# Gated linear attention followed by a sine MLP: the MLP's first weight fetched in four column quarters, with a new instruction order

## The chip, the cores and the metric

The kernel runs on one core of a Trainium2 chip. The metric is the device time of one execution in microseconds (us), as the median of several runs; lower is better. A profile of one execution comes with it, and all times inside the program are counted from the start of its span.

## The reference

Two stages follow each other. The first is a recurrence over 768 time steps for 4 batches of 8 heads with head size 48; its output, put token by token (3072 tokens of 384 numbers), goes through an MLP whose activation is `h + sin(alpha*h)^2 / alpha`.

```
f = 1 / (1 + exp(-f_logit))                       # [4, 8, 768, 48]
for t in range(768):
    state = f[:, :, t, :, None] * state + k[:, :, t] (outer) v[:, :, t]
    y[:, :, t] = q[:, :, t] @ state
x = y as [3072, 384]
h = x @ w_in                                      # [3072, 2048]
g = h + sin(alpha * h)^2 / (alpha + 1e-9)
out = g @ w_out                                   # [3072, 384]
```

## The kernel before

The sequence is cut into six chunks of 128 steps. Within a chunk the recurrence is turned into matrix products: sums of log gates (`cs`, a product with a triangular mask), the scaled `k` and `q` (`kh` and `qh`, both in the tile `qk`), their transposes (`tp`, copied to `tr`), the masked score matrix (`aps`, masked into `at`), the product with `v` (`y`, copied to `yn`), and the state carried to the next chunk (`kv`, `st`). `y` is transposed once more (`yt`, copied to `xT`) and is then the input of the MLP for the 512 tokens of this chunk (128 steps of 4 batches).

The work of `pre` is done for two batches at a time; such a unit is `u = 2*chunk + pair`, so u 0 and 1 are chunk 0, u 2 and 3 are chunk 1, and so on. A unit needs four inputs `f`, `k`, `q`, `v`, each a 384 KB DMA issued by the SyncE queue (SP) in the order that the list `LOADS` gives. Below, v2 means the `v` input of unit 2. `kh`, `qh`, `tp`, `tr`, `aps`, `at` and `kv` are made for one batch at a time, numbered m = 2*u + 0 or 1: kh2 and kh3 come from k1, kh4 and kh5 from k2. Each kind of input has three buffers.

The MLP of a chunk has 16 blocks of 128 hidden columns (`fb`). For each block: three matmuls into `h` (`first`, L543), the sine on ScalarE (L548), the square on GpSimd, ScalarE or VectorE (L554, L556), and the sum into `g` on VectorE (L561). In chunk 0 the blocks are done for two batches (256 tokens) at a time, so that chunk 0 has 32 of them; h0 to h15 are those of its first two batches. `second` multiplies `g` with `w_out` (L581) into `o`, which is copied to `osb` and stored. `h` has three PSUM buffers in turn; in chunk 0 some of the first 15 blocks use the two buffers of `o` as well.

The weights come over the GpSimd queue (POOL), since they are cast from float32 to bfloat16 on the way. Each group of these DMAs is gated: a copy of one element of an input tile into `seen` (L286) waits until that input has landed, and the DMAs stand behind it in the POOL queue. `W_GATE` tells which entries of `LOADS` are the gates of the first part of `w_in`, of its second part, and of `w_out`. In the kernel before, one half of `w_in` is three DMAs, one for each 128 rows, and a block of the second half (`fb` 8 to 15) needs all three of its half:

```python
W_GATE = [4, 7, 14]
w_in_dma[hf].append(op(rank, {POOL: 600}, emit, deps=[gate], dma=1660))
needs = lambda half, fb: [...] + w_in_dma[fb // 8]
```

The order of the instructions on every engine is made while the program is built. `op` records each operation with a rank, the engines that it may run on with a planned cost, and what it depends on; `in_order` then plays them through with these costs and takes again and again the operation that can start first, rank and `BIAS` deciding ties. So planned costs and ranks set which engine does a copy or a square, and the place of every instruction. The result is a fixed order on each engine, and on the chip each engine works its own queue in that order. `PHASES` sets when ScalarE turns between exponentials and sines, which takes a table load (L643).

Of the kernel before, what the change touches and what calls it, by code (L numbers as in the profile page):

```python
# [22 lines left out]
LOADS = [("f", 0), ("k", 0), ("q", 0), ("f", 1), ("q", 1), ("v", 0), ("k", 1), ("v", 1), ("q", 3),  # L23
    ("f", 2), ("v", 2), ("f", 3), ("k", 4), ("q", 2), ("k", 2), ("v", 3), ("k", 3), ("f", 4),
    ("f", 5), ("v", 4), ("q", 4), ("v", 7), ("q", 5), ("f", 7), ("k", 5), ("k", 6), ("v", 5),
    ("q", 8), ("f", 6), ("f", 8), ("q", 6), ("k", 7), ("v", 6), ("k", 8), ("v", 8), ("v", 10),
    ("v", 9), ("k", 10), ("q", 7), ("f", 10), ("v", 11), ("q", 10), ("f", 11), ("k", 9), ("q",
    9), ("k", 11), ("q", 11), ("f", 9)]
W_GATE = [4, 7, 14]
LAG = [1259, 664, 156, 107, 352, 821]  # L30
ATT = [816, -410, -264, -308, -540, 67]
# [3 lines left out]
RANK = [57, 902, -416, 116, 324, -1107, 154, -228, -393, 499, -57, -21]  # L35
MULS = {"POOL": 1020, "DVE": 750}
KIND = {"v": [-253, -197, -275, -90, -19, -113, 54, -23, 294, 108, -136, 11],
        "cs": [166, -99, 466, 468, 497, 525, 156, 73, 308, 100, -174, -211],
        "kh": [-420, -288, -109, -60, -261, -416, 1, 112, -116, -353, -597, -410],
        "qh": [39, -59, -267, -207, -95, -105, -79, -204, -36, -58, 106, 145],  # L40
        "tp": [-704, -587, -407, -250, -350, -423, -529, -434, -209, -113, -630, -619],
        "tr": [676, 683, 605, 574, 597, 434, 658, 637, 516, 502, 841, 893],
        "a": [-193, -33, -307, -268, -491, -499, -415, -297, -236, -148, -542, -369],
        "m": [382, 244, 882, 926, 455, 521, 870, 880, 558, 664, 209, 409],
        "y": [359, 281, 782, 934, 738, 726, 967, 789, 882, 759, 797, 900],
        "yt": [338, 442, 591, 498, 369, 453, 920, 776, 936, 571, 725, 839],
        "xe": [164, 118, 474, 430, 628, 568, 660, 448, 819, 638, 731, 791],
        "i": [-178, -9, -130, -85, -385, -454, -347, -676, -80, 105, -145, 51],
        "kv": [105, 140, -54, 56, 130, -66, -209, -24, 56, 108, 260, 93],
        "st": [-156, -144, -34, 68, -433, -296, -147, -222, -33, 60, -123, -22],  # L50
        "h": [-282, -193, -192, -427, -22, -104, -640, -227, -306, -284, -211, -314],
        "sq": [110, -5, -368, -360, -77, -233, -538, -538, -402, -388, -227, -18],
        "g": [-196, -86, -99, -320, -310, -185, -65, -203, 63, 30, -333, -448],
        "ev": [98, 89, -544, -601, -357, -242, -98, -190, -420, -283, -225, -463]}
ON_ACT = {"tr": [164, -107, -316, 43, -634, 114, -467, 93, 3854, -711, -8369, -5250],
          "y": [-1550, -3600, -3600, -14550, -10950, -650, 1050, -4550, -350, -5050, 3650, 100],
          "xe": [5550, 6200, -5450, 2700, 200, -100, 4250, 6900, 4000, 6850, 2600, 2800],
          "sq": [200, 900, 10400, -1400, -450, 450, -100, -1000, -250, 7250, -250, 12600],
          "ev": [7850, 12700, 3150, 2350, 850, 50, -5400, -700, 3000, 9250, 8600, -1850]}
BIAS = {"ACT": 500, "DVE": 500, "POOL": 600, "SP": 200}  # L60
# [25 lines left out]
def in_order(ops, lines):  # L86
# [28 lines left out]
    while left:  # L115
# [20 lines left out]
        if o.dma:  # L136
            dma_free[e] = max(s + 600, dma_free[e]) + o.dma
            o.end = dma_free[e] + DMA_LATENCY
            if e == "POOL":
                dma_free["SP"] = max(s + 600, dma_free["SP"]) + o.dma  # L140
# [18 lines left out]
def kernel(  # L159
# [18 lines left out]
    nc = tc.nc  # L178
# [38 lines left out]
    def op(rank, engs, emit, deps=(), takes=(), holds=(), table=None, dma=None):  # L217
        o = Op(rank, engs, emit, [d for d in deps if d is not None], list(takes), table, dma)
        for b in list(takes) + list(holds):
            b.users.append(o)  # L220
        ops.append(o)
        return o
# [55 lines left out]
    HF = [slice(0, d_ff // 2), slice(d_ff // 2, d_ff)]  # L278
# [3 lines left out]
    w_in_dma, w_out_dma = {0: [], 1: []}, {}  # L282
# [6 lines left out]
    def w_in_load(hf, rank):  # L289
        gate = weights_after(hf, rank)  # L290
        for kb in range(KB):
            def emit(e, kb=kb):
                nc.gpsimd.dma_start(out=w_in_bf[:, kb, HF[hf]], in_=moe_w_in[kb * P:(kb + 1) * P, HF[hf]])
            w_in_dma[hf].append(op(rank, {POOL: 600}, emit, deps=[gate], dma=1660))
# [27 lines left out]
    def pre(u, rank):  # L322
# [15 lines left out]
        l = op(rank, {ACT: 790}, ln_, deps=[x], takes=[lf], holds=[fb_], table=EXP)  # L338
        act = [x, l]
        made["v", u] = op(rank + KIND["v"][u] + 2, {DVE: 870}, values, deps=[vb_.ready], takes=[vv], holds=[vb_])  # L340
        late = []
        for i in range(2):
# [34 lines left out]
            c_ = op(rank + KIND["cs"][u] + i, {PE: 170 if last else 370}, cs_, deps=[l], takes=[cb], holds=[lf])  # L377
# [8 lines left out]
            made["qh", m] = op(rank + KIND["qh"][u] + i, {DVE: 490}, qm, deps=[g, qb_.ready], takes=[qkb], holds=[qb_, cb])  # L386
            if not last:
                made["gl", m] = op(rank + i, {DVE: 110}, gl_, deps=[g], takes=[glb], holds=[cb])
# [3 lines left out]
    def attend(c, b, rank):  # L392
# [96 lines left out]
        if c < PE_TR:  # L489
            kt = op(rank + KIND["tp"][u], {PE: 250}, lambda e: tp_(e, 0), deps=[made["kh", m]], takes=[tpb], holds=[qkb])  # L490
            qt = op(rank + KIND["tp"][u], {PE: 250}, lambda e: tp_(e, 1), deps=[made["qh", m], kt], holds=[tpb, qkb])
            tr = op(rank + KIND["tr"][u], {DVE: 640, ACT: 970}, tr_, deps=[qt], takes=[trb], holds=[tpb])
            tr.on_act = ON_ACT["tr"][u]
        else:
            tr = op(rank, {SP: 1300}, tr_, deps=[made["kh", m], made["qh", m]], takes=[trb], holds=[qkb], dma=3000)
        a = op(rank + KIND["a"][u], {PE: 400}, a_, deps=[tr], takes=ab + atb, holds=[trb])
        ms = [op(rank + KIND["m"][u], {DVE: 640}, lambda e, r=r: m_(e, r), deps=[a], holds=[ab[r], atb[r]]) for r in range(2)]
        last_ = None
        if not first:
            last_ = op(rank + KIND["i"][u], {PE: 210}, inter_, deps=[a, made["st", c - 1, b]], takes=[yb], holds=[trb, sold])  # L500
        for r in range(2):
            last_ = op(rank + KIND["i"][u], {PE: 170}, lambda e, r=r: intra_(e, r), deps=[ms[r], last_, made["v", u]],
                       takes=[yb] if first and r == 0 else [], holds=[yb, atb[r], vb])
        y_op = op(rank + KIND["y"][u], {DVE: 520, ACT: 430}, y_, deps=[last_], takes=[ynb], holds=[yb])
        y_op.on_act = ON_ACT["y"][u]
        if c < Y_TR:
            yt = op(rank + KIND["yt"][u], {PE: 200}, yt_, deps=[y_op], takes=[ytb], holds=[ynb])
            made["x", c, b] = op(rank + KIND["xe"][u], {DVE: 300, ACT: 440}, x_, deps=[yt], takes=[xb], holds=[ytb])
            made["x", c, b].on_act = ON_ACT["xe"][u]
        else:  # L510
            made["x", c, b] = op(rank + KIND["xe"][u], {SP: 1300}, yt_, deps=[y_op], takes=[xb], holds=[ynb], dma=1200)
        if not last:
            sold_op = made.get(("st", c - 1, b))
            if c < SUM:
                kv = op(rank + KIND["kv"][u] + 1, {PE: 200 if first else 370}, kv_, deps=[made["kh", m], made["v", u], sold_op],
                        takes=[kvb, sb], holds=[qkb, vb] + ([sold] if sold else []))
                made["st", c, b] = op(rank + KIND["st"][u] + 1, {DVE: 520}, st_, deps=[kv, made["gl", m]],
                                      holds=[sb, kvb, bufs["gl", m]])
            else:
                kv = op(rank + KIND["kv"][u] + 1, {PE: 200}, kv_, deps=[made["kh", m], made["v", u], sold_op],  # L520
                        takes=[kvb, sumb, sb], holds=[qkb, vb])
                su = op(rank + KIND["st"][u] + 1, {DVE: 520}, sum_, deps=[kv, sold_op], holds=[sumb, kvb, sold])
                made["st", c, b] = op(rank + KIND["st"][u] + 1, {POOL: 800, DVE: 710}, st_, deps=[su, made["gl", m]],
# [4 lines left out]
    def first(c, fb, ts, rank, needs):  # L528
# [39 lines left out]
        s = op(rank, {ACT: 455 if half else 645}, sin_, deps=[a, made["al"]], takes=[sb], holds=[hb], table=TRIG)  # L568
        t = op(rank + KIND["sq"][w], {POOL: 640 if half else 1040, ACT: 420 if half else 640, DVE: 520 if half else 917}, sq, deps=[s], takes=[s2b], holds=[sb])
        t.on_act = ON_ACT["sq"][w]  # L570
        made["g", c, fb, ts.start] = op(rank + KIND["g"][w], {DVE: 420 if half else 685}, add, deps=[t], takes=[gb], holds=[s2b, hb])
        return s

    def second(c, t, rank):
# [18 lines left out]
        v_ = op(rank + KIND["ev"][2 * c + t // 2], {DVE: 520, ACT: 500}, ev, deps=[prev], takes=[sbuf], holds=[ob])  # L593
# [17 lines left out]
    needs = lambda half, fb: [made["x", 0, 2 * half + i] for i in range(2)] + w_in_dma[fb // 8]  # L611
# [63 lines left out]
```

## Time and profile before

| What | us |
|---|---|
| median of 4 runs | 220.51 |
| the runs | 219.59 to 221.26 |
| the profiled execution's own time | 221.26 |
| its span, first to last instruction | 219.6 |
| TensorE (PE) busy | 182.9 |
| VectorE (DVE) busy | 160.2 |
| ScalarE (ACT) busy | 163.6 |
| GpSimd (POOL) busy | 100.3 |
| DMAs of `w_in`, issue to landing, shortest / median / longest | 4.7 / 7.2 / 8.1 |

The profiled execution is the slowest of the four runs, 0.75 us over the median; 1.66 us of its own time lie outside the span. The busy times are sums over the whole span: what a wait costs has to be read where it stands. "q1" in the lists of DMA queues is the queue that SP fills (inputs, stores, DMA transposes), "q0" is the one that POOL fills (`alpha`, `w_in`, `w_out`); their columns are packets, MB written, and the time of the packets as a share of the 16 DMA engines in that stretch, which exceeds 100% where packets overlap.

### The profile page before, as it was taken

Reading aid. Unit: us, or ns where it says so; the run is one execution under the profiler, and the core shown is the slowest. Engines: PE = TensorE matmul, PEld = TensorE weight load, DVE = VectorE, ACT = ScalarE, POOL = GpSimd, SP = SyncE. Lnnn points to the kernel's source line nnn. Section 1 sums busy time; section 2 is a strip of 40 time slices with the busy share of each in tenths; the row PEclk is TensorE's granted clock in tenths of the full one; section 3 lists DMA queues with packets and bytes.
Section 4 is the critical chain, followed back from the end, with each engine's and each line's share of the span. In section 5 each row is a group of like instructions: output and inputs, shape, how many; then the busy total and the mean of one; then the engine's idle time right before and its main releaser. Section 6 shows DMA issues by size and latency. Waiting matters only on the chain.

```text
span 219.6 us, 4284 instructions
## 1 busy us (share of the span) xinstructions
PE 182.9 (83%) x1537; PEld 108.0 (49%) x1537; DVE 160.2 (73%) x297; ACT 163.6 (75%) x269; POOL 100.3 (46%) x129
## 2 busy tenths in 40 slices
PE   0468545845999997896999988997999999999993
PEld 0347423524677564454565444554554555555551
DVE  2387762827689579988968998849899968787820
ACT  3565443897578997699998898998898888687601
POOL 5332441848255358867566645377604312302300
PEclk9999955755699999999999999999999999999999
DMA  7999999999998999979949999486302211001121
GB/s 130 187 188 189 181 174 180 190 202 190 210 186 161 200 184 181 186 113 188 222 93 138 187 186 217 127 159 130 109 18 40 91 25 69 0 36 72 37 74 72
DMA packets 118997, 30.30 MB, mean 138 GB/s; under 512 B 113072, under 2 KB 118208, under 8 KB 118976
## 3 DMA queue, kind: packets, MB, share of 16 engines
q1 hardware_dynamic: 115968, 26.88, 69.3%
q0 software_dynamic: 3008, 3.15, 9.2%
q8 instruction: 12, 0.20, 0.4%
q14 instruction: 9, 0.07, 0.1%
HBM read 25.17 MB, written 4.72 MB: 136 GB/s over the span
## 4 chain that ended last, share of the span: by engine, by line
PE 49%; ACT 13%; DVE 10%; issue 8%; POOL 7%; SPq 5%; DMA 5%; POOLq 0%; ACTq 0%
PE o L581 23%; PE h L543 19%; POOL s L556 6%; SPq L270 5%; DMA v<-in_v_dram 5%; DVE g L561 5%; ACT s L548 3%; ACT L643 3%; ACT Gi L364 2%; DVE at L429 2%; PE aps L426 2%; ACT lf L331 1%; ACT f L328 1%; PE tp L409 1%; ACT cs L360 1%
## 5 line engine op out<-in xcount | busy, mean ns | idle before, releaser
L556 POOL TENSOR_TENSOR s<-s 128x512 f32<-128x512 f32 (+1 forms) x67 | 58.8, 893 | 68.6 <-ACT s L548 44.0
L548 ACT ACTIVATE s<-h,al_p 128x512 f32<-128x512 f32 (+1 forms) x112 | 67.7, 626 | 27.8 <-PE h L543 23.3
L543 PE MATMUL h<-xT,w_in_bf 128*128 128x512 bf16 (+1 forms) x336 | 79.5, 362 | 10.4 <-DMA w_in_bf<-in_moe_w_in_dram 6.0
L561 DVE SCALAR_TENSOR_TENSOR g<-s,al_r,h 128x512 bf16<-128x512 f32 (+1 forms) x112 | 72.2, 667 | 10.7 <-POOL s L556 6.8
L581 PE MATMUL o<-w_out_bf,g 128*128 128x384 bf16 x384 | 78.5, 329 | 0.0
L543 PEld LDWEIGHTS <-w_in_bf 128*128 128x128 bf16 x336 | 33.1, 102 | 37.4 <-DMA w_in_bf<-in_moe_w_in_dram 7.3
L581 PEld LDWEIGHTS <-g 128*128 128x128 bf16 x384 | 35.7, 98 | 23.5 <-issue 0.7
L429 DVE TENSOR_TENSOR at<-aps,mask 128x512 bf16<-128x512 f32 x48 | 31.7, 684 | 5.0 <-PE aps L426 4.8
L373 POOL TENSOR_TENSOR qk<-k,Gi 128x384 bf16<-128x384 f32 x22 | 21.9, 1015 | 22.3 <-ACT Gi L364 19.9
L373 DVE TENSOR_TENSOR qk<-q,cs 128x384 bf16<-128x384 f32 x24 | 13.1, 552 | 13.2 <-ACT cs L360 12.5
L554 ACT ACTIVATE s<-s 128x512 f32<-128x512 f32 (+1 forms) x34 | 20.8, 614 | 0.8
L351 PE MATMUL cs<-lf,mask 128*128 128x384 bf16 x24 | 8.6, 377 | 9.8 <-ACT lf L331 8.6
L446 PE MATMUL y<-vb,at 128*128 128x48 bf16 x192 | 11.5, 187 | 4.7 <-DVE vb L335 2.8
L409 PE MATMUL tp<-ident,qk 128*128 128x128 bf16 x128 | 12.2, 259 | 3.3 <-POOL qk L373 1.9
L446 PEld LDWEIGHTS <-at 128*128 128x128 bf16 x192 | 8.9, 98 | 10.9 <-DVE at L429 5.2
L643 ACT ACT_TABLE_LOAD x11 | 14.1, 1283 | 0.2
L328 ACT ACTIVATE f<-f 128x768 f32<-128x768 f32 x12 | 10.1, 838 | 5.1 <-DMA f<-in_f_logit_dram 5.0
L556 DVE TENSOR_TENSOR s<-s 128x512 f32<-128x512 f32 (+1 forms) x11 | 7.8, 708 | 7.7 <-ACT s L548 7.6
L364 ACT ACTIVATE Gi<-cs 128x384 f32<-128x384 f32 x24 | 11.6, 485 | 2.0 <-PE cs L354 1.9
L426 PE MATMUL aps<-tr 64*128 64x128 bf16 x192 | 11.0, 229 | 2.5 <-ACT tr L417 1.5
L417 ACT COPY tr<-tp 128x1024 bf16<-128x1024 bf16 x10 | 9.9, 1019 | 3.9 <-PE tp L409 3.9
L409 PEld LDWEIGHTS <-qk 128*128 128x128 bf16 x128 | 10.4, 118 | 4.9 <-POOL qk L373 2.6
(54 smaller groups left out, 155.9 us busy)
## 6 DMA issues: line engine op xcount, KB each, us to landing
f<-in_f_logit_dram SPq DMA_DIRECT2D x12, 384.0 KB, 7.3
k<-in_k_dram SPq DMA_DIRECT2D x12, 384.0 KB, 6.6
q<-in_q_dram SPq DMA_DIRECT2D x12, 384.0 KB, 6.7
v<-in_v_dram SPq DMA_DIRECT2D x12, 384.0 KB, 6.7
out_dram<-osb SPq DMA_DIRECT2D x24, 192.0 KB, 2.1
w_in_bf<-in_moe_w_in_dram POOLq DMA_DIRECT2D x6, 256.0 KB, 7.2
w_out_bf<-in_moe_w_out_dram POOLq DMA_DIRECT2D x4, 384.0 KB, 6.6
xT<-yn SPq DMA_TRANSPOSE x12, 2.3
```

The source lines that it names most:

```text
L364: nc.scalar.activation(out=tl["Gi", m], in_=tl["cs", m][:, :H * D], func=Act.Exp)
L373: engine[e].tensor_mul(qk_b[bufs["qk", m].place % NQ][:, "kq".index(n), :, :, :D], tl[n, u][:, i * H:(i + 1) * H, :].rearrange("c (r p) d ...
L409: nc.tensor.transpose(tl[x, "tp"][:, j * HP + p, :], qk_b[qkb.place % NQ][:, j, p, :, :].rearrange("c r e -> c (r e)"), ident)
L429: nc.vector.tensor_mul(tl[x, "at", r], tl[x, "a"][r], mask4)
L446: nc.tensor.matmul(tl[x, "y"][:, h * D:(h + 1) * D], tl[x, "at", r][:, p, :], v_b[vb.place % NV][:, i, h, :], start=(first and p == r == 0 ...
L543: nc.tensor.matmul(h[:, :n], w_in_bf[:, kb, fs], xT[:, ts.start // C:ts.stop // C, kb, :], start=(kb == 0), stop=(kb == KB - 1))
L548: nc.scalar.activation(out=s[:, :n], in_=tl[x, "h"][:, :n], func=Act.Sin, scale=al_p[:, fb:fb + 1])
L554: nc.scalar.activation(out=s2[:, :n], in_=s[:, :n], func=Act.Square)
L556: engine[e].tensor_mul(s2[:, :n], s[:, :n], s[:, :n])
L561: nc.vector.scalar_tensor_tensor(tl["g", c, fb][:, ts], tl[x, "s2"][:, :n], al_r[:, fb:fb + 1], tl[x, "h"][:, :n], Alu.mult, Alu.add)
L581: nc.tensor.matmul(tl["o", c, t], tl["g", c, fb][:, t * P:(t + 1) * P], w_out_bf[:, fb, :], start=(fb == 0), stop=(fb == FB - 1))
L643: nc.scalar.preload_act_table_set(now)
```

## The change

`w_in` is loaded in four DMAs. Each takes all 384 rows of a quarter of the hidden columns (512 of 2048) as one transfer of 128 partitions x 3 x 512. A block `fb` needs only the DMA of its quarter, `fb // 4`. The first two quarters stand behind the first gate and the other two behind the second; each quarter has its own rank. The gates are now entries 4, 5 and 12 of `LOADS` (f1, q1 and f3; before q1, v1 and k2), and `LOADS` itself is another list. The planner counts a DMA of the POOL queue as landing 1500 ns later than before. Planned costs of many operations, `BIAS`, and all lists of ranks (`LAG`, `ATT`, `RANK`, `KIND`, `ON_ACT`) have new numbers. No operation of the computation is added or removed, but its place, and in some cases its engine, can differ.

```diff
-LOADS = [("f", 0), ("k", 0), ("q", 0), ("f", 1), ("q", 1), ("v", 0), ("k", 1), ("v", 1), ("q", 3),
-    ("f", 2), ("v", 2), ("f", 3), ("k", 4), ("q", 2), ("k", 2), ("v", 3), ("k", 3), ("f", 4),
+LOADS = [("f", 0), ("k", 0), ("q", 0), ("v", 0), ("f", 1), ("q", 1), ("k", 1), ("v", 1), ("f", 2),
+    ("q", 3), ("q", 2), ("k", 3), ("f", 3), ("k", 2), ("v", 2), ("v", 3), ("f", 4), ("f", 5),
...
-W_GATE = [4, 7, 14]
-LAG = [1259, 664, 156, 107, 352, 821]
-ATT = [816, -410, -264, -308, -540, 67]
+W_GATE = [4, 5, 12]
+LAG = [944, 1270, 670, 148, 173, 1651]
+ATT = [458, 340, -414, -399, -628, 476]
...
-BIAS = {"ACT": 500, "DVE": 500, "POOL": 600, "SP": 200}
+BIAS = {"ACT": 300, "DVE": 600, "POOL": 800, "SP": -15300}
...
-            o.end = dma_free[e] + DMA_LATENCY
+            o.end = dma_free[e] + DMA_LATENCY + (1500 if e == "POOL" else 0)
...
-    HF = [slice(0, d_ff // 2), slice(d_ff // 2, d_ff)]
-    w_in_dma, w_out_dma = {0: [], 1: []}, {}
+    w_in_dma, w_out_dma = {}, {}
...
     def w_in_load(hf, rank):
         gate = weights_after(hf, rank)
-        for kb in range(KB):
-            def emit(e, kb=kb):
-                nc.gpsimd.dma_start(out=w_in_bf[:, kb, HF[hf]], in_=moe_w_in[kb * P:(kb + 1) * P, HF[hf]])
-            w_in_dma[hf].append(op(rank, {POOL: 600}, emit, deps=[gate], dma=1660))
+        for n in (2 * hf, 2 * hf + 1):
+            def emit(e, fs=slice(n * d_ff // 4, (n + 1) * d_ff // 4)):
+                nc.gpsimd.dma_start(out=w_in_bf[:, :, fs], in_=moe_w_in[:, fs].rearrange("(kb p) f -> p kb f", p=P))
+            w_in_dma[n] = op(rank + 0.1 * n, {POOL: 780}, emit, deps=[gate], dma=2500)
...
-    needs = lambda half, fb: [made["x", 0, 2 * half + i] for i in range(2)] + w_in_dma[fb // 8]
+    needs = lambda half, fb: [made["x", 0, 2 * half + i] for i in range(2)] + [w_in_dma[fb // 4]]
```

The lists `RANK`, `KIND`, `ON_ACT` and the rest of `LOADS` are replaced as a whole, and some two dozen planned costs move (a `cs` product from 370 to 275, a square on VectorE from 917 to 820, the cast of `v` from 870 to 770).

## The prediction

> **What bounds the kernel now.** I read the page first, by slices of 5.5 us, for where TensorE is not yet full.
>
> ```profile
> PE   0468545845999997896999988997999999999993
> ACT  3565443897578997699998898998898888687601
> PEclk9999955755699999999999999999999999999999
> DMA  7999999999998999979949999486302211001121
> ```
>
> From about 55 us on TensorE is nearly full and its work is fixed (1537 matmuls, before and after). So time can be won in the first 55 us, where it is busy about half and where everything that comes later by x us pushes the full part by x. In the table by stretches (columns: us, then busy time and count of PE, PEld, DVE, ACT, POOL, then clock, DMA, GB/s) one stretch is empty on all engines but not on the DMA:
>
> ```profile
> 30.00:35.00 5.00, 0.79 (x2) 0.21 (x2) 1.57 (x5) 0.55 (x2) 0.05 (x1) 0.50 1.04 183
> 35.00:40.00 5.00, 4.22 (x20) 3.02 (x21) 2.47 (x6) 2.84 (x6) 2.42 (x4) 0.50 1.01 174
> ```
>
> The waits between 20 and 45 us name the cause, and the timeline its place:
>
> ```profile
> ACT s L548 <- PE h L543: 8.2, 9, 5.7
> POOL seen L286 <- DMA v<-in_v_dram: 5.9, 1, 5.9
> PE h L543 <- DMA w_in_bf<-in_moe_w_in_dram: 6.0, 4, 3.3
> ```
>
> ```profile
> 24.97 0.60 POOL L293 DMA_DIRECT2D w_in_bf<-in_moe_w_in_dram  x1
> 26.43 0.59 POOL L293 DMA_DIRECT2D w_in_bf<-in_moe_w_in_dram  x1
> 27.61 0.59 POOL L293 DMA_DIRECT2D w_in_bf<-in_moe_w_in_dram  x1
> ...
> 35.78 4.45 PE L543 MATMUL h<-xT,w_in_bf 128*128 128x256 bf16 x20 [1.02 <-DMA w_in_bf<-in_moe_w_in_dram]
> ...
> 42.30 1.28 ACT L643 ACT_TABLE_LOAD   x1
> ```
>
> The gate of the second half waits for v1 until 24.85; its three DMAs, with squares between them on POOL, land at 30.7, 34.4 and 35.8, and h8 needs all three. ScalarE makes ten more sines and loads its table at 42.30. That table load is my milestone.
>
> **The change: the transfers.** Of the DMA queues in 17 to 19 us, then in 47 to 48 us (a `w_out` DMA):
>
> ```profile
> q0 software_dynamic: 166, 0.31, 100.7%
> q1 hardware_dynamic: 2, 0.00, 0.2%
> ```
>
> ```profile
> q0 software_dynamic: 263, 0.20, 131.6%
> q1 hardware_dynamic: 6, 0.00, 0.9%
> ```
>
> POOL's queue moves 0.16 to 0.20 MB/us whatever its packet size (2 KB, 0.75 KB), and SP's queue stands still meanwhile. A quarter is 0.393 MB: 2.0 to 2.5 us. The Trainium skill (DMA: Bandwidth & Descriptors, Queues, rings and completion order) says that a DMA engine goes round the queues that have work, one packet of some 9 to 17 descriptors at a time. By equal turns SP would keep moving and the four quarters would be stretched by some 15%, an estimate; the rows show SP nearly stopped. I take the rows and keep 1 us more for the last quarter.
>
> Order of the changed program: POOL has gate f1, quarter 0, gate q1, quarters 1 to 3 back to back, then kh3. f1 is now the fifth load, the place of q1 before, whose gate ended at 13.51; q1 is the sixth, as v0 was, landed at 15.6. Four issues at 0.81 us (the `w_out` rows) cost 3.2 against six at 0.58, 3.5: nothing. From issue to first packet took 2.0 us (24.97 to 27.0) to 2.8 (13.63 to 16.4, in the queue's rows per us). With 2.8: quarter 0 moves from 16.4 and lands at about 19.5 (landing comes about 1 us after the last packet); the others follow without a gap and land at 21.6, 23.7 and 26, against 22.5 and 35.8. Only k1 matters behind them on SP: before, its last packets moved in 16 to 17 us, so it is just through.
>
> **The change: what is late next.** w_in then waits for nothing; VectorE becomes the limit of this stage. Its queue from the second qh (ending about 21.3, since the exponentials of u1 end on ACT at 20.7): kh2 0.55, two gl 0.3, tr2 0.69, four at at 0.64, 2.6, eighteen g at 0.476, 8.6, cast of v 0.7, two st 1.1, one square 0.4: 15.0 us. Two holes, for tp2 (1.0) and aps2 (0.6). It ends at 37.9. ScalarE's last sine is one sum earlier, so the table load comes at about 37.5 in place of 42.30: 4.8 us earlier. ScalarE's own queue from 21.9 (18 sines 8.6, one tr 1.0, two yn and two xT 1.9, wait for tp3 1.6, wait for y2 1.5) ends at 36.5 and agrees.
>
> **The change: does it carry on?** From this table load to the next takes 8.25 us (42.30 to 50.55), unchanged. It needs inputs 4.8 us sooner. SP resumes at 25.5 with v1 and a load each 2.05 us: f2 29.6, q3, q2, k3 35.8, f3 38, k2 40, v2 42, and lands 0.5 later. f3 at 38.5 is just in time for the second exponential (39.5). The `w_out` gate is f3, with two DMAs at once after it: first packets 41.3, until 45.4; v2 stands still meanwhile and lands at 46.3, or, if the other two `w_out` DMAs follow without a gap, at 50.5. On VectorE the cast of v2 stands in front of qh6, qh7, st and the first at of chunk 1; on TensorE kv0 waits for it, and all matmuls are behind kv0. Before, kv0 was at 52.98 and the first at at 58.34. With v2 at 46.3 they can be at 47.2 and 49.5, with 50.5 at 51.4 and 53.7: both hold the 4.8 us to within 0.2. So this wait I cost at nothing; what covers it is the late start of chunk 1 before.
>
> **The change: the rest.** By the order of instructions VectorE gives up two tr (1.4), three xT (1.0) and four osb (2.2) and takes two squares (1.5): 3.1 us less; ScalarE takes these copies (2.0 + 1.4 + 1.9) and gives up six squares (3.2): 2.1 more; POOL has four squares more, 3.0. In 70 to 160 us VectorE is 0.84 busy and ScalarE 0.89, so neither sign follows. TensorE's idle time from 80 to 160 us is 7.6 us (8.30 to 9.94 busy of each 10); another order may win or lose a third of it: 0, with 2.5 to both sides. The end is the same: from chunk 4 on both orders have the same matmuls in front of each h, to a few.
>
> Clock: the granted clock fell to 0.50 at 27.5 us, before the hole, when TensorE was busy 0.50 of 24 to 26 us. The skill (TensorE: Matmul & The Clock Gate, Part 1) gives half rate after an idle window of about 3.4 us and full rate after a busy one. By the rule, closing the hole would spare the half rate of 28 to 40 us, 6.6 us busy, so 3.3 us of matmuls; by the row the clock was gone without the hole. TensorE isn't the limit there, so I count nothing, and up to 2 us for the lower end.
>
> **Sum.** 221.26 - 4.8 = 216.5 for the profiled execution, which was 0.75 above its median; against 220.51 that is 215.7, and with 0.2 for VectorE's lighter load 215.5.
>
> **The rivals.**
> 1. More is won: the clock stays up, or the new order closes a third of TensorE's later holes: another 2 to 3.5 us, 212 to 213.5. For it: VectorE's 3.1 us. Chance 0.12, beside 0.51 for the forecast (214 to 217).
> 2. Half is lost in later holes, by ScalarE's 2.1 us in front of sines: 217 to 219.4. Chance 0.15.
> 3. The start is not earlier: with the short delay of 2.0 us quarter 0 moves at 15.6, with some 800 of k1's 2064 packets still to go; k1 is parked until the quarters end, and lands at 26. kh2 heads VectorE's queue and kh3 POOL's; the 16.6 us start at 26: table load at 42. 219.4 to 221.6. Against it: the first DMA before had 2.8. Chance 0.07.
> 4. Slower: v2 is starved. If all `w_out` DMAs run before v2, from 41.3, and each stretches to 2.8 us as the second did before, v2 lands at 53.8 to 55 where it was cast at 39.8 before; kv0 stops TensorE's queue until then. It decides from 52 us (the cast takes 0.7, and kv0 was at 52.98); with 55 the full part starts 2.7 us later than before: 223.2. For it: the rows in which SP stands still. Against it: two of the four `w_out` DMAs stand behind kh4 and kh6 on POOL. Chance 0.15.
>
> **The numbers.** A difference of about 0.5% can be told from none. Faster by more: 0.51 + 0.12 + 0.15 = 0.78; within: 0.07; slower: 0.15. The range goes from 212 (rival 1) to 222, cutting the most of rival 4.
>
> **What would show it.** Right: first packets of quarter 0 near 16.4, k1 landed by 18, no wait of h on w_in over 1 us, VectorE without a hole of more than 2 us from 22 to 38, table load at 37 to 38, first at of chunk 1 before 54. Wrong: kh2 or kh3 waiting for k1; the cast of v2 or kv0 waiting beyond 52; or the milestone reached and TensorE's holes from 80 to 160 us grown by more than 3 us.

## The result and the profile after

The changed kernel takes 219.1 us (median; 217.34 to 221.43), the kernel before, measured beside it, 220.03 (218.18 to 222.02). The ratio is 0.9951, with an interval of 0.9935 to 0.9967: 0.9 us faster, where 215.5 was predicted. The profiled execution of after has an own time of 220.58 us and a span of 218.9; for before these were 221.26 and 219.6.

First the answer to what was shown of before. By slices of the page, after:

```profile
PE   0477885589969999858899987989999999999993
ACT  3578589967587979896998999686788888667711
PEclk9999999559996999988999997999999999999999
DMA  7999999999999999789799994815611211010211
```

In before TensorE was at 4 to 8 tenths from 5 to 55 us and then nearly full; it has low digits there too (7 at 82 to 88 us, 6 at 99 to 104), but its granted clock has no dent behind 60 us. In after it is at 7 to 8 from 11 to 33 us, but has new low digits at 60 to 66 us (6), 93 to 99 (5) and 131 to 137 (7), each with a dent in its granted clock there or just behind (6, 8 and 8, 7), far behind the stage in which w_in arrives. The table by stretches (columns as before) for the two stretches in which before stood still:

```profile
30.00:35.00 5.00, 4.16 (x49) 2.77 (x48) 4.72 (x12) 4.21 (x11) 3.42 (x6) 1.00 1.13 188
35.00:40.00 5.00, 2.26 (x19) 1.39 (x19) 1.31 (x3) 4.91 (x7) 2.86 (x5) 0.87 1.26 194
```

The hole is closed: TensorE 4.16 busy of 5 us instead of 0.79. The timeline of after shows the transfers, the only wait of `h` for them that is left, and the milestone:

```profile
13.45 0.17 POOL L285 COPY seen<-f 1x1 f32<-1x1 f32 x1 [3.60 <-DMA f<-in_f_logit_dram]
13.57 0.82 POOL L292 DMA_DIRECT2D w_in_bf<-in_moe_w_in_dram  x1
15.56 0.17 POOL L285 COPY seen<-q 1x1 f32<-1x1 f32 x1 [1.18 <-DMA q<-in_q_dram]
15.68 2.32 POOL L292 DMA_DIRECT2D w_in_bf<-in_moe_w_in_dram  x3
...
19.57 1.46 PE L542 MATMUL h<-xT,w_in_bf 128*128 128x256 bf16 x6 [1.25 <-DMA w_in_bf<-in_moe_w_in_dram]
...
35.36 1.28 ACT L642 ACT_TABLE_LOAD   x1
```

Quarter 0 is there at 19.57, as forecast (19.5), and no block waits for the other three. The table load stands at 35.36 instead of 42.30: a lead of 6.9 us, more than the 4.8 of the forecast. So the lead came, and went. Each table load of ScalarE is a fixed point of the program that both kernels have; the table gives the start of eight of them in us, and the lead is before minus after. "Sine 96" is the 97th of the 112 sines. The profiled executions of before and of after are both slower than the medians of their kernels (221.26 against 220.03, 220.58 against 219.1), so a lead between two traces is good to a microsecond or two against the medians; what tells is where it changes.

| Table load ahead of | before | after | lead | old order, new transfers (first experiment) | its lead |
|---|---|---|---|---|---|
| exponentials of u 2 and 3 | 42.30 | 35.36 | 6.9 | 35.93 | 6.4 |
| the 14 sines behind these | 50.55 | 44.67 | 5.9 | 44.18 | 6.4 |
| exponentials of u 4 and 5 | 69.19 | 61.77 | 7.4 | 62.44 | 6.8 |
| exponential of u 6 | 93.22 | 86.29 | 6.9 | 86.44 | 6.8 |
| exponentials of u 7 and 8 | 106.54 | 101.65 | 4.9 | 99.76 | 6.8 |
| the 16 sines behind these | 115.71 | 109.90 | 5.8 | 108.94 | 6.8 |
| exponentials of u 9 to 11 | 135.49 | 130.90 | 4.6 | 128.71 | 6.8 |
| the last 48 sines | 147.03 | 144.56 | 2.5 | 140.26 | 6.8 |
| sine 96 (no load) | 188.45 | 187.72 | 0.7 | 181.67 | 6.8 |

The row of the 16 sines splits the loss. From this load to the end before takes 103.85 us, the old order with the new transfers takes the same 103.85, and after takes 109.0. So 5.1 of the 6.1 us between the spans of the last two (218.9 and 212.8) are lost behind it. From the load ahead of the last 48 sines to the end, after and then the old order with the new transfers:

```profile
144.56:218.90 74.34, 69.74 (x492) 37.77 (x490) 54.23 (x82) 51.28 (x82) 22.95 (x23) 1.00 0.22 63
140.26:212.80 72.54, 67.65 (x461) 36.09 (x459) 53.17 (x81) 51.44 (x82) 20.18 (x21) 0.99 0.23 61
```

Before needs 72.5 us here as well. After is 1.8 us longer, since TensorE has more left to do: counted in the traces, 208 `o` matmuls start behind this load against 196 in the other two. At the load ahead of the 16 sines it is 298 against 272. So the table flatters after: where ScalarE leads, TensorE has put work off.

### The profile page after: what moved, and what is told of

The parts are those of the page before. It is cut to its first block, busy times and chain, and to the rows that moved or that the text cites. A ratio compares the mean times of both kernels' runs of the same rounds, so it can differ in the third digit from the quotient of the medians.

```text
span 218.9 us, 4268 instructions
## 1 busy us (share of the span) xinstructions
PE 186.1 (85%) x1537; PEld 108.6 (50%) x1537; DVE 157.2 (72%) x290; ACT 165.9 (76%) x272; POOL 102.5 (47%) x131
## 3 DMA queue, kind: packets, MB, share of 16 engines
HBM read 25.17 MB, written 4.72 MB: 137 GB/s over the span
## 4 chain that ended last, share of the span: by engine, by line
PE 59%; DVE 14%; DMA 9%; ACT 6%; issue 5%; POOL 3%; SPq 3%; ACTq 0%; POOLq 0%; DVEq 0%
PE o L580 25%; PE h L542 24%; DVE g L560 6%; DMA f<-in_f_logit_dram 3%; DMA v<-in_v_dram 3%; DMA w_in_bf<-in_moe_w_in_dram 3%; POOL s L555 3%; SPq L270 3%; PE tp L408 2%; DVE at L428 2%; PE aps L425 2%; DVE vb L334 2%; PE cs L350 2%; PE y L445 2%; ACT s L547 1%
## 5 line engine op out<-in xcount | busy, mean ns | idle before, releaser
L555 POOL TENSOR_TENSOR s<-s 128x512 f32<-128x512 f32 (+1 forms) x71 | 61.0, 874 | 64.4 <-ACT s L547 56.6
L580 PE MATMUL o<-w_out_bf,g 128*128 128x384 bf16 x384 | 79.6, 333 | 2.5 <-DVE g L560 2.3
L542 PEld LDWEIGHTS <-w_in_bf 128*128 128x128 bf16 x336 | 32.8, 101 | 32.2 <-issue 9.4
L553 ACT ACTIVATE s<-s 128x512 f32<-128x512 f32 x28 | 17.6, 633 | 0.7
L350 PE MATMUL cs<-lf,mask 128*128 128x384 bf16 x24 | 9.3, 405 | 10.1 <-ACT lf L330 9.0
L416 ACT COPY tr<-tp 128x1024 bf16<-128x1024 bf16 x12 | 12.1, 1014 | 3.6 <-PE tp L408 3.5
L485 POOL TENSOR_TENSOR st<-sum,gl 128x384 bf16<-128x384 f32 x12 | 10.3, 862 | 5.3 <-DVE sum L481 5.3
L425 PEld LDWEIGHTS <-tr 64*128 64x128 bf16 x192 | 6.2, 99 | 11.8 <-issue 6.0
```

The lines of the kernel that those rows point to most:

```text
L425: nc.tensor.matmul(aps[r][:, p, :], t[halves[r], p, :], t[halves[r], HP + p, :], start=True, stop=True)
L542: nc.tensor.matmul(h[:, :n], w_in_bf[:, kb, fs], xT[:, ts.start // C:ts.stop // C, kb, :], start=(kb == 0), stop=(kb == KB - 1))
L553: nc.scalar.activation(out=s2[:, :n], in_=s[:, :n], func=Act.Square)
L555: engine[e].tensor_mul(s2[:, :n], s[:, :n], s[:, :n])
L580: nc.tensor.matmul(tl["o", c, t], tl["g", c, fb][:, t * P:(t + 1) * P], w_out_bf[:, fb, :], start=(fb == 0), stop=(fb == FB - 1))
```

## The experiments

In all of them the order of the instructions on every engine is written out as a fixed list. "Old order" is the list of before, "new order" that of after; the diffs give the queues. The w_in transfers are called halves (six DMAs, as before) or quarters (four, as after).

**1. Apart: the transfers without the order, and the order without the transfers.** Before, measured beside these, takes 219.24 us (218.51 to 220.59). The first kernel has only the POOL queue's transfers changed:

```diff
 every engine: old order
-POOL: gate q1, three DMAs of half 0, ... gate v1, three DMAs of half 1 among squares
+POOL: gate q1, quarter 0, gate v0, quarters 1, 2, 3
```

> The instruction order of the kernel before, fixed, with only the transfers of w_in changed: quarter 0 behind q1, quarters 1 to 3 back to back behind v0. In the new kernel the second table load of the chunk-0 sines came 6.9 us earlier than before (35.4 against 42.3), and only 0.7 us was left at the end. Theory A (the new order of instructions loses the lead later, by waits of TensorE and the half clock after them): with the old order the lead is kept; v1 is parked behind the quarters and its cast stands in front of the g on VectorE, so the lead at the table load is about 3 us, and the run is 2 to 3 us faster than before, 217 to 218. Theory B (the later stages take the lead back in any order, since ScalarE and VectorE set their pace): the lead at the table load is there and the end is within 1 us of before, 219.5 to 220.5.

Measured: 214.44 us (214.34 to 214.51), ratio 0.9774 (0.9728 to 0.982). By medians that is 4.8 us less than before, the size that was forecast for the transfers (between the two profiled executions, 221.26 and 214.5, it is 6.8, since the one of before is 2 us over the median here). The last column above shows it carried without loss: 6.8 us at every table load from that ahead of u 4 on. The loss at the table load that Theory A expected of the parked v1 did not come (35.93 us, a lead of 6.4 and not 3), so the run is below its 217 to 218. Its median is the lowest of all versions, and it beats both kernels.

The counterpart has the new order with the halves:

```diff
 every engine: new order, SP with v1 right behind k1
-POOL: gate f1, quarter 0, gate q1, quarters 1, 2, 3
+POOL: gate f1, three DMAs of half 0, ... gate v1, three DMAs of half 1 among squares
```

> The instruction order of the new kernel, fixed, with w_in as before: three DMAs of the first half behind f1, three of the second half behind v1 with squares between them. h8 waits until about 35 again. Theory A: the new order without its early start is slower than before by what it loses later, 5 to 6 us: 224 to 226. Theory B: the end is where it was, 219.5 to 221.

Measured: 225.89 us (223.29 to 226.99), ratio 1.0256 (1.0171 to 1.0341). The new order by itself costs 6.65 us. It is not lost at the start. Its waits for w_in are about those of before:

```profile
PEld L556 <- DMA w_in_bf<-in_moe_w_in_dram: 8.6, 5, 2.5
ACT s L561 <- PE h L556: 8.6, 12, 5.0
...
PE h L556 <- DMA w_in_bf<-in_moe_w_in_dram: 6.8, 4, 2.4
```

(waits from 20 to 45 us; before had 6.0 where this has 6.8), and the table load behind them stands at 42.55 us, in before at 42.30. The two effects don't add up: -4.8 and +6.65 make +1.9, and after stands at -0.9; why the order costs less with the quarters stays open. But each sign is clear: the gain is the transfers', the loss the order's.

**2. What of the transfers brings it: their shape or their gates?** Quarters at the old gates:

```diff
 every engine: old order
-POOL: gate q1, three DMAs of half 0, ... gate v1, three DMAs of half 1 among squares
+POOL: gate q1, quarters 0, 1, ... gate v1, quarters 2, 3
```

> The order of before, fixed, and its gates (q1 and v1); two quarters behind each gate, issued without squares between them. h12 can start at about 32 where h8 started at 35.8: table load about 3.5 us earlier than 42.3. Theory A: 3 us faster than before, about 217. Theory B: 219.5 to 220.5.

Measured: 215.1 us (214.19 to 216.65), ratio 0.9811 (0.9746 to 0.9876), some 2 us less than Theory A had. And the reverse, the halves at the early gates:

```diff
 every engine: old order
-POOL: gate q1, three DMAs of half 0, ... gate v1, three DMAs of half 1 among squares
+POOL: gate q1, three DMAs of half 0, gate v0, three DMAs of half 1
```

> The order of before, fixed, with w_in in the six old DMAs, by halves, but early: three behind q1 and three back to back behind v0. It separates the earlier gate from the shape by quarters. The second half lands at about 27 in place of 35.8 and the first at 22.5. If the earlier start is what counts: as old_order_new_w (214.4), within 1 us. If blocks that wait for their quarter alone are needed: 216 to 218.

Measured: 217.26 us (216.02 to 218.13), ratio 0.9888 (0.9832 to 0.9943; before 219.69 beside it). By medians the quarters give most of the gain even at the late gates and the early gates alone about half of it; the two intervals overlap a little. What holds the halves back is in the waits of that kernel from 15 to 40 us:

```profile
PE y L459 <- DVE vb L348: 6.2, 2, 5.0
DVE vb L348 <- DMA v<-in_v_dram: 4.1, 2, 3.5
```

The six DMAs in a row park v1 on SP's queue; its cast waits 3.5 us, and `y` behind it 5.0. In the first experiment, with the same early gates, the casts of `v` together waited 2.6 us, at most 1.1.

**3. Where the new order loses: a hole in front of chunk 1's sines.** From 60 to 70 us, after, and then the old order with the quarters (table by stretches):

```profile
60.00:65.00 5.00, 3.11 (x42) 2.40 (x42) 5.00 (x13) 4.04 (x7) 1.31 (x3) 1.00 1.20 198
65.00:70.00 5.00, 4.78 (x27) 2.24 (x27) 0.93 (x4) 3.58 (x7) 0.56 (x1) 0.66 1.36 187
```

```profile
60.00:65.00 5.00, 5.00 (x61) 3.47 (x59) 4.85 (x11) 4.78 (x9) 2.36 (x4) 1.00 1.24 188
65.00:70.00 5.00, 5.00 (x45) 2.94 (x44) 2.60 (x8) 4.87 (x10) 1.96 (x2) 1.00 1.28 220
```

The timeline of after names the waits:

```profile
62.64 0.79 PE L465 MATMUL yt<-ident,yn 128*128 128x128 bf16 x6 [0.51 <-DVE st L485]
64.33 0.33 PE L465 MATMUL yt<-ident,yn 128*128 128x128 bf16 x3 [0.90 <-ACT xT L468]
65.22 3.21 PE L542 MATMUL h<-xT,w_in_bf 128*128 128x512 bf16 x9 [0.57 <-ACT xT L468]
```

TensorE waits for one transpose after the other, though `o` matmuls of chunk 0 are ready: in the new order they are queued behind the first three `h` and the `cs`. In the old order `o` products stand between these transposes. So eight of them were put ahead:

```diff
 new order, quarters
-PE: ... yt yt yt yt h h h cs cs cs o o o o o o o o ...
+PE: ... o o o yt yt o o o yt yt o o h h h cs cs cs ...
 VectorE: the copy of the first o tile earlier, so that its PSUM buffer is free
```

> The new kernel with one piece of order changed: eight matmuls of o for the third token tile of chunk 0 are put ahead of the last transposes of chunk 1 and its first h on TensorE, where it stands still 2 us at 62 to 65 us and then runs at half clock until 68 us; the copy of the first o to osb goes ahead on VectorE so that its buffer is free. Theory A: up to 3 us faster than the new kernel, 216 to 217.5. Theory B, or if VectorE (busy 5.0 of 5 us there) is what holds this stage: within 0.7 us of it, or slower, since the transposes come later.

Measured: 216.93 us (216.2 to 218.16), ratio 0.9891 (0.9822 to 0.9961). That is where Theory A had it, but the interval overlaps with that of after (0.9935 to 0.9967), so the gain is not proven. In its profile TensorE is 4.19 busy in 60 to 65 instead of 3.11, the clock stays at 1.00 in 60 to 75 and in 95 to 100, and the lead at sine 62 (126 us) is 8.0 instead of 4.7. The half clock in 65 to 70 could itself have been the loss. So after was run with 14 matmuls without use in the hole:

```diff
 new order, quarters
-PE: ... yt yt yt yt h h h ...
+PE: ... (4 idle) yt yt (6 idle) yt yt (4 idle) h h h ...
```

> The new kernel with 14 matmuls of 256 columns added on TensorE into a buffer of h that is overwritten after, 4, 6 and 4 of them at the three waits between 61 and 65 us; nothing else moves. It separates the wait from the half clock behind it. If the half clock at 65 to 68 us costs what it stretches (three h of chunk 1 took 3.21 us where 2.0 is their time at full clock), the first sine of chunk 1 comes about 1 us earlier and the run is 0.5 to 1.2 us faster than the new kernel. If only the wait counts, or the clock falls all the same: equal within 0.5 us, or up to 1.5 us slower by the added matmuls.

```profile
60.00:65.00 5.00, 4.79 (x72) 3.96 (x67) 4.89 (x12) 4.21 (x8) 2.48 (x5) 1.00 1.18 198
65.00:70.00 5.00, 4.79 (x41) 2.79 (x39) 2.69 (x8) 4.82 (x10) 1.01 (x2) 1.00 1.23 182
```

The clock held here, and the time is 218.14 us (216.55 to 219.57), ratio 0.9967 (0.9921 to 1.0014): no gain that can be told from after's 0.9951. The interval is too wide to exclude the 0.5 to 1.2 us that were expected, and the two later dents of the clock (at 95 and 133 us) are still in this profile. So it doesn't show that the half clock costs nothing; it shows that holding the clock in this one place does not bring back the some 4 us that after takes over the old order with the quarters.

**4. Where the new order loses: by parts.** Two kernels join the orders at the first `h` of chunk 1 (some 44 us), two at the exponential of unit 7 (some 100 us); all have the quarters. (Before, beside them: 220.07.)

```diff
 every engine
-new order
+old order up to the join, then the new order with what is left
```

> The reverse: the old order up to the first h of chunk 1, then the new one, with the new quarters. Theory A: the loss comes all the same, 217.5 to 220. Rival B: most of the loss is gone, 214 to 216.

> Old order up to the exponential of unit 7 (some 100 us), then the new order. Theory A: the late part of the new order loses its 4 to 6 us here too: 217.5 to 220. If the loss was made before 100 us (work put off): 214 to 216. If each half bears a part: about 216.5 in this and in the run before.

Measured: 218.07 us (216.65 to 219.15), ratio 0.9901 (0.9863 to 0.9939) with the join at 44, and 218.44 us (217.36 to 219.6), ratio 0.9933 (0.9895 to 0.997), with the join at 100. Against 0.9774 for the old order all through (measured beside other runs of before), the part behind 44 us costs 1.3% and the part behind 100 us, which is inside it, 1.6%: within their intervals the same, some 3 us, so that this loss lies behind 100 us. The leads say so too: the join at 100 has 6.9 us at sine 62, about what the old order has, and 3.9 at sine 96. The part up to 44 us costs less (0.9951 against 0.9901, 1.1 us, and these two intervals touch). The reverse joins were run too:

> The new quarters in all four kernels of this call. Here the new order up to the first h of chunk 1 (some 44 us), then every engine goes on in the old order with what is left. With the old order all through and the same quarters it was 214.4, with the new order all through 219.1. Theory A (the new order loses in its late part, after some 90 us, where the lead of the table loads falls from 6.9 to 0.7 us): the lead is kept to the end, 214 to 216. Rival B (the new order's first part leaves less of the o products done and the later stages pay for it, whatever their order): 217.5 to 219.5.

> New order up to the exponential of unit 7 (some 100 us), then the old order. Theory A: nearly all of the lead at that point (6.8 us) reaches the end: 214.5 to 216.5. Rival B, or a loss that is made before 100 us and only shows at the end (work put off): 217.5 to 220.

Measured: 221.1 us (219.81 to 222.06), ratio 1.0073 (1.0044 to 1.0101), and 224.91 us (223.63 to 225.15), ratio 1.022 (1.0161 to 1.0279). Both are slower than any of the theories had them, and read by these alone, the old order would be the bad part. But the joins make waits that neither kernel has: of the first, from 55 to 80 us, and of the second, from 100 to 140 us:

```profile
DVE vb L347 <- DMA v<-in_v_dram: 4.7, 1, 4.7
```

```profile
ACT Gi L376 <- PE cs L366: 3.0, 1, 3.0
PE h L555 <- DVE g L573: 3.0, 4, 2.3
```

The list of loads is joined with the rest, and an input comes when neither order had it come. So the times of these two say nothing of the halves of the order, and the two forward joins may owe a part of theirs to the joining as well.

The ends of the traces do say something. From the load ahead of u 9 to 11 to the end, the six kernels that end in the old order (before, the three of parts 1 and 2, the two reverse joins) all take 84.06 to 84.07 us, whatever they did earlier; the ten that end in the new order take 85.8 to 88.1. From the last load it is 72.5 us in all six, and 74.3 in nine of the ten, with 196 and 208 `o` matmuls left. So every kernel with the new end loses at least 1.7 us there. Twelve `o` matmuls are about as long: 1.9 us, an estimate from their spacing of 0.16 us in after at 190 us.

Another join at 44 us, with the `o` products ahead, took 216.83 us, ratio 0.9875; it leaves out waits, so that some operands of the attention products are written over before their last reader, and nothing is concluded from its time:

> The new kernel with the o matmuls moved ahead (new_o2_ahead) up to its first h of chunk 1, and from there the remaining instructions in the order of the kernel before. new_o2_ahead was 8.8 us ahead of before at the first sine of chunk 1 and lost 4.6 us of it by the end of chunk 3; the old order with new transfers kept its 6.8 us to the end. Theory A (what is lost is lost by the new order of chunks 1 to 3): about 8 us of lead are kept, 211.5 to 213.5. Theory B' (the lead above 6.8 us can't be kept, since the old order meets other limits then): 214 to 215. If the join costs a wait of its own: 215 to 218.

**5. What in the late part loses.** From 126 to 134 us, in turn after, the old order with quarters, and the old order to 100 us with the new one behind it:

```profile
126.00:134.00 8.00, 5.96 (x38) 2.59 (x36) 6.92 (x11) 7.61 (x11) 1.87 (x2) 1.00 1.08 160
```

```profile
126.00:134.00 8.00, 7.74 (x70) 4.37 (x68) 6.76 (x12) 7.28 (x11) 3.03 (x3) 1.00 0.72 156
```

```profile
126.00:134.00 8.00, 5.74 (x50) 2.68 (x49) 6.64 (x11) 7.72 (x12) 1.22 (x2) 1.00 0.81 138
```

TensorE is idle for 2.0 and 2.3 us against 0.3. The timeline of the third kernel has the waits:

```profile
129.44 0.50 PE L593 MATMUL o<-w_out_bf,g 128*128 128x384 bf16 x2 [0.95 <-DVE g L573]
131.22 0.50 PE L593 MATMUL o<-w_out_bf,g 128*128 128x384 bf16 x2 [0.68 <-DVE g L573]
...
128.16 0.56 DVE L347 CAST vb<-v 128x768 bf16<-128x768 f32 x1 [1.18 <-DMA v<-in_v_dram]
```

v11 is the last of all loads in the new list, and its cast stands in front of the last three `g` of chunk 2, though nothing needs it before the last chunk. Two squares of 1.09 us, which POOL does in the old order, stand there on VectorE too. First the cast was put six instructions later (the expectation counts eight, and four `g`), then the two squares were also given to POOL, and last both edits were made in the new order with the `o` products ahead (before: 220.43):

```diff
 old order to 100 us, then the new order; quarters
-DVE: ... g  s  g  g  cast v11  g  s  g  g  at  at ...
+DVE: ... g  s  g  g  g  s  g  g  at  at  cast v11 ...
```

> As old_to_100_new_on (218.44), with the cast of v11 put eight VectorE instructions later, behind the second at (v11 isn't used before the last chunk). Theory A (the wait of the cast for the last load, 1.2 us in front of four g, stops TensorE): TensorE's idle time in 126 to 134 us falls from 2.3 to some 1.2 us and 1 us comes off the end: 217.0 to 217.8. Rival B (the hole comes from VectorE's whole load in this stretch, and the wait is only where it shows): 218.0 to 218.8.

```diff
-DVE: ... g  s  g  g  g  s  g  g  at  at  cast v11 ...
+DVE: ... g  g  g  g  g  g  at  at  cast v11 ...        POOL: two s more
```

> As the run before, and the two squares of this stretch (1.09 us each) done by POOL, which is idle there for 3.8 us, instead of VectorE. Theory C (VectorE's two squares are the rest of the hole): 215.5 to 216.8. If POOL's squares come later than VectorE's did, the g wait for them and nothing is won: 217 to 218.5.

> Both edits in the new order with the o products ahead (216.93 before). If the two causes add up, nearly all of the loss of the new order is found: 214.2 to 215.5, as the old order with the same quarters (214.44). If the early lead is lost again further on: 216.2 to 217.5.

Measured: 217.57 us (217.04 to 219.64), ratio 0.9882 (0.9841 to 0.9924), for the cast alone. It is inside what was expected of the wait, and TensorE's idle time in 126 to 134 us fell from 2.26 to 1.72 us, but the intervals overlap with 0.9933: it points that way and doesn't prove it. With the squares on POOL: 219.22 us (217.33 to 220.59), ratio 0.9964 (0.9924 to 1.0005): the gain is gone, and the table load ahead of the last sines is 3.4 us later (144.44 against 141.03). The guess on the squares found no support. The two traces don't settle it, since this one has two late stretches at half clock (at 104 and 135 us) and that of the cast alone has none. Both edits in the new order: 218.06 us (216.07 to 221.87), ratio 0.9868 (0.9816 to 0.992), no different from the `o` products alone (0.9891); the causes did not add up. The three edits together are faster than after, though: this interval and that of after (0.9935 to 0.9967) don't meet.

One more try on the late part, ahead of these: three `cs` products of units 10 and 11, which stand behind `o` and `h` in TensorE's queue while ScalarE waits for them, were put ahead.

```diff
 new order, o products ahead, quarters
-PE: ... h and o ... cs (u10) ... o ... cs cs (u11)
+PE: ... cs (u10) h and o ... cs cs (u11) o ...
```

> new_o2_ahead with three more products cs (the log-gate sums of the last two units) taken ahead of h and o on TensorE. In the new kernel the last stage of exponentials lasted 13.7 us between its table loads (11.5 before) with ScalarE waiting 2.3 us for cs behind them. Theory A (places in TensorE's queue are what loses the lead): this stage is 1 to 2 us shorter and the run 1 to 1.5 us faster than new_o2_ahead (216.9): 215.4 to 216. If TensorE's own backlog of o decides from there: within 0.5 us of it.

Measured: 218.14 us (216.88 to 220.0), ratio 0.995 (0.9905 to 0.9994). The stage of these exponentials did get shorter in its profile, 11.2 us from table load to table load instead of 13.6, but the lead that it made was gone again some 20 us later: at the last load 212 `o` matmuls are left instead of 208, and the rest takes 75.5 us. Of the some 3 us behind 100 us, 1.8 are thus found behind the last load, where more `o` is left over. Which instructions between 100 us and this load cost the rest stays open.

## Why the prediction was right or wrong

**The transfers: right.** Packets of quarter 0 were running in 17 to 19 us and it landed by 19.57; k1 was just through, `kh2` started at 18.11 without waiting for it; the only wait of `h` on w_in is 1.25 us, a little over the 1 us that was allowed. The other three quarters did not follow without a gap: their packets moved from 19.7 to some 27 us. With the old order this was worth 4.8 us by medians, as the sum had it; that the figures agree is in part luck, since the lead in the traces was 6.8 and the profiled execution of before stood 2 us over its median. The milestone was under-estimated, 35.36 instead of 37.5: VectorE did carry the stage (4.78 and 4.72 busy of 5 in 25 to 35 us), but ScalarE's last sine came three sums before VectorE's last one and not one, at 34.88, with the last `g` at 36.28.

**Who stands still when both queues have work: right for a part of the time only.** The queues of after in 17 to 19 us, in the first of these two microseconds alone, in 24 to 25 us, and in 47 to 48 us:

```profile
q0 software_dynamic: 299, 0.29, 89.6%
q1 hardware_dynamic: 706, 0.14, 33.7%
```

```profile
q0 software_dynamic: 196, 0.20, 123.1%
```

```profile
q0 software_dynamic: 165, 0.16, 93.4%
q1 hardware_dynamic: 163, 0.03, 29.1%
```

```profile
q0 software_dynamic: 189, 0.15, 92.8%
q1 hardware_dynamic: 189, 0.04, 34.6%
```

Before, the stretches at 17 and 47 us had 2 and 6 packets of SP's queue. In after SP's queue moves nothing from 17 to 18 us beside quarter 0 (it has no row there), as the prediction had it; its 706 packets come from 18 to 19, when quarter 0 ends and the next has not begun. But from 24 to 25 and from 47 to 48 us the two queues move equal numbers of packets. That fits the turn by turn of the Trainium skill (DMA: Bandwidth & Descriptors, Queues, rings and completion order), not the standstill that the prediction took from before's rows. Which of the two comes when, no run here shows. It cost nothing: SP's queue was slowed, but v2 was cast at 42.36.

**Does it carry on: right for the place that was asked about.** kv0 of chunk 1 ran at 44.35 and the first `at` at 46.69 (before 52.98 and 58.34); v2 was not starved, so rival 4 did not happen. Nor did rival 3. From the milestone to the next table load it took 9.31 us (35.36 to 44.67) and not "8.25, unchanged"; with the old order and the quarters it was 8.25.

**The rest: this is the step that failed.** The prediction costed the new order behind chunk 1's start at "0, with 2.5 to both sides", by counting the work that moves between engines and the idle time of TensorE from 80 to 160 us, and said "The end is the same". The order alone costs 6.65 us with the halves, and with the quarters after is 1.8% of the time, some 4 us, over the old order. The count itself was right: VectorE is 3.0 us less busy and ScalarE 2.3 us more (157.2 and 165.9 us, before 160.2 and 163.6), where 3.1 and 2.1 were counted. It was no guide to the time.

Nor was TensorE's idle time. From 80 to 160 us it is 8.3 us in after and was 7.6 in before, far from the 3 us more that were to be the sign of this failure. Over the whole span after is idle for 32.8 us and the old order with the quarters for 33.7. What differs is how long the same 1537 matmuls keep TensorE busy: 186.1 us against 179.1, and by the estimate below 5.1 of these 7.0 us are half clock.

"The end is the same" was wrong as well: from the 16 sines on after takes 5.1 us more, and at the last load it has 12 `o` matmuls more to do and takes 1.8 us more. The prediction compared the matmuls in front of each `h` from chunk 4 on, not what is left over from earlier chunks. One place where the sum could have seen a part of it is the order of instructions: TensorE's queue has four transposes in a row, each behind a copy of another engine, and the ready `o` behind them. Rival 2 gave the time (217 to 219.4), but by holes that ScalarE's 2.1 us make in front of sines; no run tests these 2.1 us apart.

**The clock: the prediction counted nothing for a hole that it closed, and that was right; it did not ask whether new holes bring the half clock back.** The clock's row on the page of the old order with quarters, and after by single microseconds:

```profile
PEclk9999999856999999999999999999999999999999
```

```profile
62.00:63.00 1.00, 0.46 (x6) 0.22 (x4) 1.00 (x4) 1.00 (x1) 0.08 (x1) 1.00 1.11 188
63.00:64.00 1.00, 0.33 (x3) 0.21 (x3) 1.00 (x4) 0.99 (x3) 0.00 (x0) 1.00 1.35 194
64.00:65.00 1.00, 0.33 (x3) 0.25 (x3) 1.00 (x4) 0.58 (x2) 0.00 (x0) 1.00 1.34 195
65.00:66.00 1.00, 0.78 (x4) 0.39 (x4) 0.84 (x2) 1.00 (x3) 0.00 (x0) 1.00 1.41 184
66.00:67.00 1.00, 1.00 (x5) 0.35 (x3) 0.00 (x0) 0.97 (x2) 0.00 (x0) 0.53 1.34 189
```

The half clock follows the hole by a microsecond and lasts until about 69.5: nine `h` matmuls took 3.21 us. After has three such stretches of 3.4 us behind 60 us, from 66.1, 96.8 and 134.3 us, and TensorE is nearly full in them; the old order with quarters has none. At full clock half of that busy time would have done. By this estimate the three stretches cost 5.1 us, of 6.1 between the two spans. (The split by place, 5.1 us behind the 16 sines, counts the same loss in another way; the two don't add.)

The half clock isn't the whole. The join at 100 us and the one with the cast of v11 later have no such stretch in their traces, and their spans are still 2.9 and 2.5 us over that of the old order with quarters (215.7 and 215.3 against 212.8). The runs say the same. Those of after fall into groups by mean granted clock: 220.33 us at 0.953 (17 runs), 218.55 at 0.961 (20), 217.63 at 0.968 and 0.969 (7). Those of before go from 221.08 at 0.936 and 0.937 (7) over 219.63 at 0.957 to 0.961 (34) to 217.38 and 217.96 at 0.976. So in both the time goes with the clock. But at 0.968, which both have, the old order with quarters takes 214.34 and 214.39 us and after 217.34 to 217.77. How much of the loss the order makes by holes that bring the half clock and how much by work that it puts off is not separated by any run.

## What to carry to other kernels

Ask of a change with two parts what each is worth alone: here a gain of 4.8 us in the transfers was nearly hidden by a new order that costs 6.65 by itself. A lead at one milestone is worth only what reaches the end. List the same fixed points (here the table loads) of both traces, and take from each the time to the end and the matmuls that the full engine has left: a lead of one engine can be work that another has put off. And when an order is new everywhere, don't cost it at zero because the work is the same; read the granted clock beside the idle time, read the queue of the full engine for instructions that wait on other engines with ready work behind them, and take the range wide where that can't be summed.

## What the runs showed of the hardware

- TensorE's clock was halved without a wholly idle stretch: it fell at 66.1 us after 1.12 us of work in 62 to 65, and came back 3.4 us later. Elsewhere 1.02 us of work in two microseconds (75 to 77 us in the old order with quarters) and 0.74 in three (91 to 94 us in the run with the `o` products ahead) left it at 1.00. So the same amount of work does not always decide it.
- SP's queue beside a transfer of POOL's queue stood still at one time and had equal turns at another, in one execution: 0 packets beside 196 in 17 to 18 us, 163 beside 165 in 24 to 25. A row of one execution on how two queues share the DMA engines was not a rule.
